# From tile 12 on, k joins r on the block-turned path, and two GpSimd products move to ScalarE

## The chip, the cores and the metric

One Trainium2 chip, one NeuronCore of it. The metric is the device time of one execution in microseconds (us); lower is better. Engines are named as in the profile: PE (TensorE matmuls; PEld its weight loads), DVE (VectorE), ACT (ScalarE), POOL (GpSimd), SP (SyncE, which here only issues DMAs).

## The reference

An RWKV-like attention (batch 4, 8 heads, 768 steps, head size 48) feeds a mixture of 8 experts whose gate is balanced by eight Sinkhorn rounds.

```python
state = 0                                   # per batch and head, 48 x 48
for t in range(768):
    y[t] = r[t] @ (state + (u * k[t]) outer v[t])
    state = w[:, None] * state + k[t] outer v[t]
x = y as (3072, 384)
P = sinkhorn(exp(x @ w_gate - max))         # 3072 x 8
out = sum over e of P[:, e] * (relu(x @ w1[e]) @ w2[e])   # 384 -> 1024 -> 384
```

## The kernel before, in words

The 3072 tokens are 24 tiles of 128; six tiles make one batch entry. The decays are handled in chunks of one tile: r and k are multiplied by tables of powers of w, so that inside a tile attention is a masked product, and between tiles only a state (`sd`, copied into `S`) is handed on.

The main loop runs `for i in range(NTT + 3)`; a pass of it is called iteration i below. In iteration i every engine gets its instructions in program order (each call goes through a wrapper that forbids reordering), and the engines meet only at semaphores. What iteration i issues, in this order:

- loads of k, r, v for tile i+4 on SP (`load_round`); `prep(i+2)`: r and k of tile i+2 times tables, into `rp_` and `kp_`; from tile 12 on (`TX0 = 12`) r takes another way, below;
- `bonus_dot(i+1)`: on POOL, `rk` = r times k, then times u;
- `stage_b(i+1)`: PE turns tile i+1 (four 128x128 transposes each for r and k, tiles `prT`, `pkT`), ACT copies them to `rT`, `kT`;
- `bonus(i)`: DVE sums `rk` by heads into `dg`, POOL forms `av` = v times `dg`;
- `sum_x`, `scale_x(i-2)`: ACT takes the sum of absolute values of the attention output `x`, DVE turns it into a power-of-two scale (`inv_s`, `xs`), ACT writes the high half `xsc`;
- `spread(i-1)`: ACT copies the state `sd` into `S`;
- `work(1)`: one unit of expert 0 on PE, either a `g1` unit (9 matmuls into `ph`; ACT forms the high half of relu, `hb`, and DVE the low half, also `hb`) or a `g2` unit (12 matmuls from `hb` into `po`; ACT copies to `stg`, SP stores it to `e0d`);
- `stage_c(i)`: PE forms scores `pA` from `kT` and `rT`, DVE masks them into `at`; the low half of the unit above comes after that on DVE; PE forms the state's update `pu`, DVE adds it to `sd`, POOL multiplies `sd` by the decay of a tile (`wcb`);
- `low_x(i-2)`: DVE forms the low half of `xsc`, SP transposes it by DMA into `hbx`;
- `work(2)`: two more expert units;
- steps of `combine_tokens` (`prepare`): DVE sums `ws<-hbx`, POOL sums `ws<-ws`, ACT casts and DVE low halves `xv`, four SP copies `xv<-hbx` every six iterations;
- `stage_d(i-1)`: PE forms `py`; `finish(i-1)`: DVE adds `py` and `av` into `x`;
- `load_blocks(i+4)`; `stage_f(i-4)`: PE forms gate logits `px`, ACT copies them to `lparts`.

So the PE order of an iteration is: transposes, unit, `pA`, `pu`, two units, `py`, `px`. PSUM buffers that matter: `ph` has two, `po` and `px` share two (`tag="po"`), and `pA`, `pu`, `py`, `prT`, `pkT` share four.

The other way of r, from tile 12 on: `load_blocks` reads r again by four DMAs (each block of 32 steps twice, shifted) into `rx_`; `turn_r` transposes 32x32 blocks on DVE into `rp_`; `scale_r` multiplies by `tab` on POOL and writes `rT`. There are two `rx_` buffers, and `turn_r` of tile i+2 stands in `prep(i+2)`, early in iteration i.

After the loop come the other seven experts, with fewer matmuls by a 3x3 bilinear scheme (`bA`, `bB`, `bC`, `bY`, `bZ`), and a general path that these inputs do not take.

Of the kernel before, what the change touches and what calls it, by code (L numbers as in the profile page):

```python
# [8 lines left out]
F32 = mybir.dt.float32  # L9
# [3 lines left out]
AF = mybir.ActivationFunctionType  # L13
ALU = mybir.AluOpType
# [19 lines left out]
def rwkv_sinkhorn_moe(  # L34
# [47 lines left out]


    HB = FHC * TH * TB // 2
    hbx = const.tile([P, 3 * HB], F32, name="hbx")
# [238 lines left out]
    RX = GX * D + 32  # L324
    rx_ = [part(hbx, F32, 3 * HB - (2 - i) * NPAIR * RX, (NPAIR, RX)) for i in range(2)]

    def load_blocks(tt):
        b, c = divmod(tt, NCHB)
        src = r[b].rearrange("(p j) (n q g) d -> j n q p (g d)", j=2, g=GX, q=32)
        for j in range(2):  # L330
            for lo in (0, 32):
                rows = slice(HP * j + lo, HP * j + lo + 32)
                Q.dma_start(rx_[tt % 2][rows, :, 32 - lo : 32 - lo + GX * D], src[j, c])
# [84 lines left out]
    tabr, tab = (part(hb3, F32, at_, (NPAIR, C)) for at_ in (1040, HB))  # L418
# [52 lines left out]
    def turn_r(tt):  # L471
        x_ = rx_[tt % 2][:, :, 32:].rearrange("p a (g d) -> p a g d", d=D)[:, :, :, :32]
        V.transpose(rp_[tt % 2].rearrange("p (a j) (g q) -> p a (j g) q", j=2, q=32), x_)

    def scale_r(tt):
        rT = at2.tile([P, NPAIR, P], F32, tag="rT", name=f"rT_{tt}", bufs=3)
        x_ = rp_[tt % 2].rearrange("p (a j) (g q) -> p a q (j g)", j=2, q=32)
        G.tensor_tensor(
            rT.rearrange("p a (q g) -> p a q g", g=GX), x_,
            tab.rearrange("p a (q g) -> p a q g", g=GX), op=ALU.mult,  # L480
        )
        st.setdefault(tt, {})["rT"] = rT

    def prep_r(tt):
        if tt >= TX0:
            turn_r(tt)
            return
        G.tensor_tensor(rp_[tt % 2][:, :, :D], loads[tt]["r"], rt4, op=ALU.mult)

# [30 lines left out]
    def bonus(tt):  # L520
        vn = loads[tt]["v"]
        dg = at2.tile([P, H], F32, tag="dg", name=f"dg_{tt}")
        V.tensor_reduce(dg, st[tt]["rk"], axis=AX.X, op=ALU.add)
        av = st[tt].pop("rk")
        G.tensor_tensor(av, vn, dg.unsqueeze(2).broadcast_to([P, H, D]), op=ALU.mult)
        st[tt]["av"] = av

    def stage_b(tt):
        d = st.setdefault(tt, {})
        for nm, src in (("rT", rp_[tt % 2]), ("kT", kp_[tt % 3]))[tt >= TX0 :]:  # L530
            pt = ps3.tile([P, NPAIR, P], F32, tag="pa", name=f"p{nm}_{tt}")
# [277 lines left out]
    for i in range(NTT + 3):  # L809
        if i == 1:  # L810
            gate_max()
        if i + 2 < NTT:
            if i != 4:
                load_round(i)
            if i:
                if i + 1 >= TX0:
                    scale_r(i + 1)
                prep(i + 2)
        elif i + 1 < NTT:
            scale_r(i + 1)  # L820
# [33 lines left out]
        held[0] = False  # L854
        form_lows()
        if i == 4:
            for x_ in rx_:
                G.memset(x_[:, :, GX * D :], 0.0)
# [20 lines left out]
        planned(i, "c")  # L879
        for _ in range(n_steps(i, 1)):  # L880
            prepare()
        if 1 <= i <= NTT:
            stage_d(i - 1)
            if i > NSUM:
                finish(i - 1)
        if i > NSUM:
            planned(i, "d")
            for _ in range(n_steps(i, 2)):
                prepare()
        if TX0 <= i + 4 < NTT:  # L890
# [586 lines left out]
```

## Time and profile before

| | |
|---|---|
| runs | 1513.76, 1515.78, 1516.59 us; median 1515.78 |
| profiled execution | 1516.68 us, its span 1514.7 us; granted clock 0.999 |
| busy over the span | PE 99%, PEld 56%, DVE 66%, ACT 46%, POOL 37% |
| chain that ended last | PE 95%, DVE 2%, SP's queue 1%, DMA 1% |
| tiles 12 to 23 | iterations 12 to 23: first `pA` at 98.8 us, last `py` ends near 211 us |

All instructions carry one line number (a helper records them), so rows are told apart by engine, tile names and shapes. A row of the timeline reads: start in us, length in us, engine, operation, out<-in, shape, and in brackets how long the engine had been idle and what ended that. A row of groups ends in: busy us, mean ns | idle us before. Spacing between starts is used where instructions of an engine overlap.

### The profile page before, as it was taken

To read this page: it belongs to the slowest core of one execution; us is meant where nothing else is said; L and a number is where in the kernel's file an instruction comes from. 1 tells how busy PE (TensorE), PEld (TensorE's weight loads), DVE (VectorE), ACT (ScalarE), POOL (GpSimd) and SP (SyncE) were. 2 spreads that over 40 slices of the span, in tenths; PEclk is the share of its full clock that TensorE was granted. 3 is DMA by queue.
4 is the path that set the end of the run, shared out by engine and by line. 5 is a ranking of instruction groups with operands and counts; after the bars stand their busy time and mean duration, and the time that the engine had idled before them with its cause. 6 is when DMAs were issued, how large, how long until landed. Compare 5 with 4: busy or idle time off the path is not lost.

```text
span 1514.7 us, 26043 instructions
## 1 busy us (share of the span) xinstructions
PE 1502.9 (99%) x10228; PEld 847.8 (56%) x10228; DVE 995.2 (66%) x1647; ACT 696.9 (46%) x1289; POOL 565.9 (37%) x667
## 2 busy tenths in 40 slices
PE   8999999999999999999999999999999999999998
PEld 6777666555555555555555555555555555555555
DVE  6878759576666666666676666666565666566563
ACT  7645545345354544445454544545353544444320
POOL 8577946200224243342525243242424233242200
PEclk9999999999999999999999999999999999999999
DMA  9776732212255566756666676655554454545434
GB/s 185 163 168 147 142 82 81 83 47 73 82 108 63 83 128 92 126 81 123 91 93 110 89 128 92 118 59 98 61 96 57 60 97 61 95 62 96 57 96 131
DMA packets 193638, 147.69 MB, mean 98 GB/s; under 512 B 110306, under 2 KB 187748, under 8 KB 193508
## 3 DMA queue, kind: packets, MB, share of 16 engines
q0 software_dynamic: 44928, 61.36, 32.7%
q1 hardware_dynamic: 148370, 84.60, 21.1%
q8 instruction: 81, 1.33, 0.4%
q14 instruction: 49, 0.40, 0.1%
q10 hardware_dynamic: 210, 0.00, 0.0%
HBM read 59.92 MB, written 80.23 MB: 93 GB/s over the span
## 4 chain that ended last, share of the span: by engine, by line
PE 95%; DVE 2%; SPq 1%; DMA 1%; ACT 0%; issue 0%; ACTq 0%; DVEq 0%
PE po L30 49%; PE bZ L30 12%; PE bY L30 12%; PE ph L30 6%; PE bA L30 5%; PE bB L30 5%; PE bC L30 2%; PE py L30 2%; PE pA L30 1%; SPq L30 1%; PE pu L30 1%; PE pkT L30 1%; PE px L30 0%; DMA ws<-in_moe_w_dram 0%; DMA hbx<-xsc 0%; DVE wms L30 0%
## 5 line engine op out<-in xcount | busy, mean ns | idle before, releaser
L30 PE MATMUL po<-ws,hbx 128*128 128x384 f16 x3360 | 737.0, 326 | 0.0
L30 POOL DMA_DIRECT2D accd<-stg x288 | 249.7, 867 | 694.9 <-ACT stg L30 670.9
L30 PEld LDWEIGHTS <-hbx 128*128 128x128 f16 x3504 | 333.9, 98 | 295.8 <-DMA hbx<-xsc 2.5
L30 PEld LDWEIGHTS <-ws 128*128 128x128 f16 x3096 | 301.4, 98 | 245.0 <-issue 2.0
L30 ACT ACTIVATE hbx<-tb 128x512 f16<-128x512 f32 x224 | 141.1, 630 | 448.6 <-DVE tb L30 448.6
L30 PE MATMUL po<-ws,hb 128*128 128x384 f16 x1248 | 323.3, 326 | 0.0
L30 DVE TENSOR_TENSOR tb<-bY,tb 128x512 f32<-128x512 f32 x168 | 116.2, 691 | 195.8 <-PE bY L30 195.4
L30 ACT ACTIVATE stg<-po,pe 128x384 f32<-128x384 f32 x312 | 179.2, 574 | 122.4 <-PE po L30 98.0
L30 PE MATMUL bZ<-xv,ws 128*128 128x512 f16 x840 | 227.1, 379 | 0.5 <-DVE tb L30 0.5
L30 PE MATMUL bY<-xv,ws 128*128 128x512 f16 x840 | 227.1, 379 | 0.0
L30 DVE TENSOR_TENSOR tb<-bZ,tb 128x512 f32<-128x512 f32 x168 | 115.6, 688 | 134.7 <-PE bZ L30 134.7
L30 PEld LDWEIGHTS <-hb 128*128 128x128 f16 x1248 | 121.3, 98 | 93.4 <-issue 0.6
L30 POOL TENSOR_TENSOR ucb<-rawb 128x256 f32<-128x256 f32 x84 | 76.9, 966 | 116.5 <-DVE tb L30 78.3
L30 DVE TENSOR_TENSOR tb<-bB,tb 128x512 f32<-128x512 f32 x112 | 77.5, 692 | 49.2 <-PE bB L30 47.3
L30 PE MATMUL ph<-hbx,ws 128*128 128x384 f16 x576 | 104.2, 326 | 0.8 <-DVE hb L30 0.8
L30 DVE SCALAR_TENSOR_TENSOR hb<-tb,hbx 128x512 f16<-128x512 f32 x112 | 77.2, 689 | 24.6 <-ACT hbx L30 19.5
L30 PE MATMUL bA<-xv,ws 128*128 128x512 f16 x336 | 90.8, 379 | 0.0
L30 PE MATMUL bB<-xv,ws 128*128 128x512 f16 x336 | 90.8, 379 | 0.0
L30 DVE SCALAR_TENSOR_TENSOR hbx<-tb,hbx 128x512 f16<-128x512 f32 x112 | 77.3, 691 | 14.6 <-ACT hbx L30 10.4
L30 ACT COPY tb<-bZ 128x512 f32<-128x512 f32 x56 | 32.7, 585 | 65.6 <-PE bZ L30 65.5
L30 DVE SCALAR_TENSOR_TENSOR hb<-ph,hb 128x384 f16<-128x384 f32 x64 | 35.3, 552 | 29.3 <-ACT hb L30 28.8
L30 DVE TENSOR_REDUCE wms<-rawb 128x1 f32<-128x768 f32 x56 | 51.7, 944 | 0.0
(177 smaller groups left out, 1460.9 us busy)
## 6 DMA issues: line engine op xcount, KB each, us to landing
accd<-stg POOLq DMA_DIRECT2D x288, 192.0 KB, 3.6
rawb<-in_moe_w_dram SPq DMA_DIRECT2D x28, 768.0 KB, 7.6
e0d<-stg SPq DMA_DIRECT2D x48, 192.0 KB, 2.1
hb<-e0d SPq DMA_DIRECT2D x48, 192.0 KB, 3.7
vn<-in_v_dram SPq DMA_DIRECT2D x24, 192.0 KB, 3.4
hbx<-in_r_dram SPq DMA_DIRECT2D x48, 96.0 KB, 2.8
accd<-stg SPq DMA_DIRECT2D x24, 192.0 KB, 1.8
accd<-hb POOLq DMA_DIRECT2D x24, 192.0 KB, 4.7
```

The lines of the kernel that those rows point to most:

```text
L30: return lambda *a, **k: self.tc.keep_in_program_order(f(*a, **k))
```

## The change

From tile 12 on:

- k too is loaded by blocks (twice, four DMAs), turned on DVE, and given its decays by a POOL product that writes `kT`; PE's transposes `pkT` and ACT's copy of them are gone. `rtab`, no longer needed as such by then, takes the table for k (one ACT multiplication in iteration 10).
- `rx_` holds k and r of one tile instead of r of two tiles; `load_blocks` is called for tile i+3 instead of i+4, at the same place of iteration i; both turns of tile i+2 stand in front of `stage_d(i-1)` instead of early in iteration i.
- `av`, v times the bonus sums, is formed by eight ACT instructions (one a head) ahead of `stage_f`, instead of one POOL product.
- the state's decay is applied by four ACT instructions in `spread`, in front of the copies into `S`, instead of one POOL product behind DVE's sum. This concerns `sd` of tiles 13 to 16 and 19 to 22.

```diff
-    def turn_r(tt): ...
-    def scale_r(tt): ...
+    def turn():
+        for dst, x_ in zip(rp_, rx_):
+            V.transpose(dst..., x_[:, 32:]...[:, :, :, :32])
+
+    def scale_turned(tt):
+        for nm, src, t_, n in zip(("kT", "rT"), rp_, (rtab..., tab), (2, 3)):
+            dst = at2.tile([P, NPAIR, P], F32, tag=nm, name=f"{nm}_{tt}", bufs=n)
+            G.tensor_tensor(dst..., src..., t_..., op=ALU.mult)
...
+    def bonus_heads(tt):
+        d = st[tt]
+        d["av"] = av = d.pop("rk")
+        for h in range(H):
+            S_.activation(av[:, h], loads[tt]["v"][:, h], AF.Copy, scale=d["dg"][:, h : h + 1])
...
     def stage_b(tt):
+        if tt >= TX0:
+            return
...
-                G.tensor_tensor(sd, sd, wcb, op=ALU.mult)
+                if tt < TX0:
+                    G.tensor_tensor(sd, sd, wcb, op=ALU.mult)
...
+            if tt >= TX0 and tt % NCHB:
+                for p_ in range(NPAIR):
+                    s_ = sd_[tt % 2][:, p_]
+                    S_.activation(s_, s_, AF.Copy, scale=wc[:, p_ : p_ + 1])
...
+        if TX0 <= i + 2 < NTT:
+            turn()
         if 1 <= i <= NTT:
             stage_d(i - 1)
...
-        if TX0 <= i + 4 < NTT:
-            load_blocks(i + 4)
+        if TX0 <= i + 3 < NTT:
+            load_blocks(i + 3)
+        if TX0 <= i < NTT:
+            bonus_heads(i)
         if 4 <= i:
             stage_f(i - 4, bank_)
```

DVE from the low half `xv` at the end of iteration 15 to the head sums `dg` of iteration 16 (`ws<-hbx` are the sums of `combine_tokens`, `STREAM_TRANSPOSE` is a turn); before:

```order
L30 TENSOR_TENSOR xv_76<-ws_74,xv_76 128x4x256
L30 TENSOR_TENSOR x_2282<-py_2257,rk_1862 128x384
L30 TENSOR_TENSOR ws_74<-hbx 128x2x3x128 x2
L30 STREAM_TRANSPOSE rp_157<-hbx 128x512
L30 TENSOR_TENSOR kp_159<-kn_1995,ktab 128x8x48
L30 TENSOR_REDUCE dg_2317<-rk_2154 128x8
```

The same stretch of DVE, changed:

```order
L30 TENSOR_TENSOR xv_76<-ws_74,xv_76 128x4x256
L30 STREAM_TRANSPOSE rp_157<-hbx 128x512
L30 STREAM_TRANSPOSE rp_158<-hbx 128x512
L30 TENSOR_TENSOR x_2312<-py_2287,rk_1879 128x384
L30 TENSOR_TENSOR ws_74<-hbx 128x2x3x128 x2
L30 TENSOR_TENSOR kp_159<-kn_2017,ktab 128x8x48
L30 TENSOR_REDUCE dg_2353<-rk_2187 128x8
```

There are two turns instead of one, and both stand ahead of `x` and of everything of the next iteration.

ACT from the cast at the end of iteration 15 to the first relu `hb` of iteration 16; before:

```order
L30 CAST xv_76<-ws_74 128x4x256
L30 ACTIVATE lparts<-px_2254,inv_s 128x16
L30 COPY kT_2315<-pkT_2310 128x512
L30 ACTIVATE xsc_2321,xm_2320<-x_2282 128x384
L30 ACTIVATE xsc_2321<-x_2282,xs_2323 128x384
L30 COPY S_165<-sd_167 64x4x48 x2
L30 ACTIVATE hb_73<-ph_2_2330 128x384
```

The same stretch of ACT, changed:

```order
L30 CAST xv_76<-ws_74 128x4x256
L30 ACTIVATE rk_2028<-vn_1575,dg_2190 128x48 x8
L30 ACTIVATE lparts<-px_2282,inv_s 128x16
L30 ACTIVATE xsc_2356,xm_2355<-x_2312 128x384
L30 ACTIVATE xsc_2356<-x_2312,xs_2358 128x384
L30 ACTIVATE sd_167<-sd_167,wc 128x48 x4
L30 COPY S_165<-sd_167 64x4x48 x2
L30 ACTIVATE hb_73<-ph_2_2369 128x384
```

Eight small instructions stand ahead of `lparts`, four ahead of the copies into `S` and so ahead of the relu; the copy into `kT` is gone.

SP's queue at the end of iteration 10, where the four copies `xv<-hbx` stand; before:

```order
L30 DMA e0d_80<-stg_0_1_1500 128x384
L30 DMA xv_76<-hbx 128x2x128 x4
L30 DMA hbx<-in_r_dram 32x4x192 x4
L30 DMA kn_1562<-in_k_dram 128x8x48
L30 DMA rn_1564<-in_r_dram 128x8x48
```

The same stretch of SP's queue, changed:

```order
L30 DMA e0d_80<-stg_0_1_1503 128x384
L30 DMA xv_76<-hbx 128x2x128 x4
L30 DMA hbx<-in_k_dram 32x4x192 x4
L30 DMA hbx<-in_r_dram 32x4x192 x4
L30 DMA kn_1571<-in_k_dram 128x8x48
L30 DMA rn_1573<-in_r_dram 128x8x48
```

Eight block loads stand there instead of four, and they are for tile 13 instead of tile 14.

More of the change, by code (lines that the diff above doesn't have):

```diff
@@ L84, in rwkv_sinkhorn_moe @@
     HB = FHC * TH * TB // 2
-    hbx = const.tile([P, 3 * HB], F32, name="hbx")
+    hbx = const.tile([P, 3 * HB + 32], F32, name="hbx")
     hb3 = const.tile([P, HB + 2 * DM], F32, name="hb3")
@@ L322, in load_part @@
         loads.setdefault(tt, {})[nm] = t_
-    RX = GX * D + 32
-    rx_ = [part(hbx, F32, 3 * HB - (2 - i) * NPAIR * RX, (NPAIR, RX)) for i in range(2)]
+    RX = NPAIR * GX * D
+    rx_ = [part(hbx, F32, 3 * HB - (2 - i) * RX, (RX + 32,)) for i in range(2)]
     def load_blocks(tt):
         b, c = divmod(tt, NCHB)
[L329 to L333, printed above, removed]
+        for x_, all_ in zip(rx_, (k, r)):
+            src = all_[b].rearrange("(p j) (n q g) d -> j n q p (g d)", j=2, g=GX, q=32)
+            for j in range(2):
+                for lo in (0, 32):
+                    rows = slice(HP * j + lo, HP * j + lo + 32)
+                    Q.dma_start(
+                        x_[rows, 32 - lo : 32 - lo + RX].rearrange("p (a d) -> p a d", d=GX * D), src[j, c]
+                    )
     raws = (part(ws0, F32, 0, (KC, F)), part(ws0, F32, KC * F, (FC, DM)))
@@ L417, in rwkv_sinkhorn_moe @@
     )
-    tabr, tab = (part(hb3, F32, at_, (NPAIR, C)) for at_ in (1040, HB))
+    tab = part(hb3, F32, HB, (NPAIR, C))
+    tabr = part(hbx, F32, 3 * HB - 2 * RX - NPAIR * C, (NPAIR, C))
     S_.copy(tab[:, :, HP:], pw[:, :, :HP])
@@ L469, in rwkv_sinkhorn_moe @@
     kt4 = ktab.rearrange("p a j d -> p (a j) d")[:, :, :D]
[L471 to L482, printed above, removed]
+    def turn():
+        for dst, x_ in zip(rp_, rx_):
+            V.transpose(
+                dst.rearrange("p (a j) (g q) -> p a (j g) q", j=2, q=32),
+                x_[:, 32:].rearrange("p (a g d) -> p a g d", g=GX, d=D)[:, :, :, :32],
+            )
+    def scale_turned(tt):
+        for nm, src, t_, n in zip(("kT", "rT"), rp_, (rtab.rearrange("p a j d -> p a (j d)"), tab), (2, 3)):
+            dst = at2.tile([P, NPAIR, P], F32, tag=nm, name=f"{nm}_{tt}", bufs=n)
+            G.tensor_tensor(
+                dst.rearrange("p a (q g) -> p a q g", g=GX),
+                src.rearrange("p (a j) (g q) -> p a q (j g)", j=2, q=32),
+                t_.rearrange("p a (q g) -> p a q g", g=GX), op=ALU.mult,
+            )
+            st.setdefault(tt, {})[nm] = dst
     def prep_r(tt):
         if tt >= TX0:
-            turn_r(tt)
             return
@@ L523, in bonus @@
         V.tensor_reduce(dg, st[tt]["rk"], axis=AX.X, op=ALU.add)
-        av = st[tt].pop("rk")
-        G.tensor_tensor(av, vn, dg.unsqueeze(2).broadcast_to([P, H, D]), op=ALU.mult)
-        st[tt]["av"] = av
+        st[tt]["dg"] = dg
+        if tt < TX0:
+            av = st[tt].pop("rk")
+            G.tensor_tensor(av, vn, dg.unsqueeze(2).broadcast_to([P, H, D]), op=ALU.mult)
+            st[tt]["av"] = av
+    def bonus_heads(tt):
[3 more added lines that the diff above has]
+            S_.activation(av[:, h], loads[tt]["v"][:, h], AF.Copy, scale=d["dg"][:, h : h + 1])
     def stage_b(tt):
+        if tt >= TX0:
+            return
         d = st.setdefault(tt, {})
-        for nm, src in (("rT", rp_[tt % 2]), ("kT", kp_[tt % 3]))[tt >= TX0 :]:
+        for nm, src in (("rT", rp_[tt % 2]), ("kT", kp_[tt % 3])):
             pt = ps3.tile([P, NPAIR, P], F32, tag="pa", name=f"p{nm}_{tt}")
@@ L575, in stage_c @@
                 V.tensor_tensor(sd, pu, sd_[(tt - 1) % 2], op=ALU.add)
-                G.tensor_tensor(sd, sd, wcb, op=ALU.mult)
+                if tt < TX0:
+                    G.tensor_tensor(sd, sd, wcb, op=ALU.mult)
     def spread(tt):
@@ L816, in rwkv_sinkhorn_moe @@
                 if i + 1 >= TX0:
-                    scale_r(i + 1)
+                    scale_turned(i + 1)
                 prep(i + 2)
         elif i + 1 < NTT:
-            scale_r(i + 1)
+            scale_turned(i + 1)
         if i + 1 < NTT and i:
@@ L824, in rwkv_sinkhorn_moe @@
             stage_b(i + 1)
+        if i == TX0 - 2:
+            S_.mul(rtab.rearrange("p a j d -> p a (j d)"), tabr, rows_used)
         planned(i, "s")
@@ L856, in rwkv_sinkhorn_moe @@
         if i == 4:
-            for x_ in rx_:
-                G.memset(x_[:, :, GX * D :], 0.0)
+            G.memset(rx_[1][:, RX:], 0.0)
+            rows_used = ac.tile([P, 1], F32, name="rows_used")
+            G.memset(rows_used, 0.0)
+            for j in range(2):
+                G.memset(rows_used[j * HP : j * HP + D], 1.0)
             load_round(i, "rk")
```

## The prediction

> **What bounds the kernel now.** I read the page first, then PE's waits in the stage that the change touches, then the timelines of DVE and ACT there.
>
> ```profile
> PE 1502.9 (99%) x10228; PEld 847.8 (56%) x10228; DVE 995.2 (66%) x1647; ACT 696.9 (46%) x1289; POOL 565.9 (37%) x667
> ...
> PE ph L30 <- DVE hb L30: 0.8, 1, 0.8
> ...
> 150.00:180.00 30.00, 30.00 (x431) 21.00 (x427) 24.32 (x47) 15.00 (x35) 29.29 (x31) 1.00 0.87 174
> ```
>
> The first row says that PE is busy for 99% of the span. The next heads the list of PE's waits between 60 and 330 us: 0.8 us, once. The last is a stretch of the stage (PE, PEld, DVE, ACT, POOL, clock, DMA share, GB/s): PE never stops, but POOL is busy for 29.3 of 30 us, DVE for 24.3, and the DMA engines for 0.87 of the time. So PE sets the pace, and the others have little to spare. Work taken off PE pays only as far as they follow.
>
> **What PE gives up.** The transposes of k, four a tile, for tiles 12 to 23:
>
> ```profile
> 186.45 0.31 PE L30 MATMUL px<-wgp,hbx 128*128 128x16 f16 x6
> 186.61 0.64 PE L30 MATMUL pkT<-ident,kp 128*128 128x128 f32 x4
> 187.08 2.11 PE L30 MATMUL po<-ws,hb 128*128 128x384 f16 x12
> ...
> 196.01 0.31 PE L30 MATMUL px<-wgp,hbx 128*128 128x16 f16 x6
> 196.18 1.62 PE L30 MATMUL ph<-hbx,ws 128*128 128x384 f16 x9
> ```
>
> With `pkT`, the next unit starts 0.63 us after `px`; without it (tile 24 doesn't exist) 0.17 us after. The lengths overlap; the place itself is 187.08 - 186.61 = 0.47 us. Twelve of them are 5.6 us, and that is all PE can gain. The profiled execution took 1516.68 us (its span and 2.0 us around it), 0.9 us over the median of 1515.78, to which I apply the sum.
>
> **What the others get.** Durations from groups over 100 to 210 us (the last two numbers before the bar's end are busy us, mean ns):
>
> ```profile
> L30 DVE STREAM_TRANSPOSE rp<-hbx 128x512 f32<-128x512 f32 x9 | 6.3, 702 | 1.2 <-POOL ws L30 0.6 <-DMA hbx<-in_r_dram 0.6
> L30 DVE TENSOR_TENSOR kp<-kn,ktab 128x384 f32<-128x384 f32 x9 | 8.1, 896 | 0.0
> L30 POOL TENSOR_TENSOR rT<-rp,hb 128x512 f32<-128x512 f32 x11 | 18.0, 1632 | 2.8 <-PE py L30 2.8
> L30 POOL TENSOR_TENSOR rk<-vn,dg 128x384 f32<-128x384 f32 x12 | 11.5, 957 | 1.0 <-DVE inv_s L30 1.0
> L30 POOL TENSOR_TENSOR sd<-sd,wcb 128x192 f32<-128x192 f32 x8 | 5.8, 720 | 4.2 <-DVE sd L30 3.2 <-ACT stg L30 1.0
> L30 ACT ACTIVATE xsc<-x,xs 128x384 f16<-128x384 f32 x13 | 8.0, 616 | 24.7 <-DVE xs L30 24.7
> L30 ACT CAST xv<-ws 128x768 f16<-128x768 f32 x5 | 4.2, 832 | 0.1
> L30 ACT CAST xv<-ws 128x1024 f16<-128x1024 f32 x2 | 2.1, 1046 | 0.1
> ```
>
> - POOL: 12 products `kT` at 1.63 (as `rT`) are +19.6; 12 `av` at 0.96 and 8 `sd` at 0.72 go, -17.2. Net +2.4 us over twelve iterations. `kT` and `rT` of tile i+1 are formed in iteration i and read by `pA` an iteration later, so I cost POOL at nothing; without that cover `kT`'s 1.6 us would stand in front of `pA`.
> - DVE: one turn more a tile. Starts below are 0.63 apart, so +0.63 an iteration.
> - ACT: the two casts give 214 ns for 256 elements, 0.84 ns each; `xsc`, which also scales by a column, comes down from 616 ns at 384 elements to 335 at 48, and its successor starts 0.09 before its end (139.86 + 0.61 against 140.38 below). So 0.245 each: 1.96 for the heads, 0.98 for four pairs of the state. The smallest bound is half of that, the largest 335 ns unoverlapped, 1.3 for four. The heads stand in front of `lparts`, behind which ACT waits for DVE's `x` anyway, beside `xv` and the two turns (1.88 and 1.26 in iteration 15, below); hidden. The copy into `kT` that goes stood in the same cover and saves nothing. The state's four are not, as follows.
>
> **Where it lands on PE.** Iteration 15 into 17, one chain over ACT and DVE beside PE:
>
> ```profile
> 131.17 0.48 ACT L30 COPY stg<-po 128x384 f32<-128x384 f32 x1 [1.50 <-PE po L30]
> ...
> 132.75 0.31 PE L30 MATMUL px<-wgp,hbx 128*128 128x16 f16 x6
> 132.75 1.88 DVE L30 TENSOR_TENSOR xv<-ws,xv 128x1024 f16<-128x1024 f32 x1 [2.49 <-ACT xv L30]
> ...
> 137.56 0.70 DVE L30 STREAM_TRANSPOSE rp<-hbx 128x512 f32<-128x512 f32 x1
> 138.19 0.72 DVE L30 TENSOR_TENSOR kp<-kn,ktab 128x384 f32<-128x384 f32 x1
> ...
> 139.86 0.61 ACT L30 ACTIVATE xsc<-x,xs 128x384 f16<-128x384 f32 x1 [4.06 <-DVE xs L30]
> 140.38 0.71 ACT L30 COPY S<-sd 64x192 f32<-64x192 f32 x2
> ...
> 141.63 0.56 DVE L30 SCALAR_TENSOR_TENSOR hb<-ph,hb 128x384 f16<-128x384 f32 x1 [0.54 <-ACT hb L30]
> ...
> 142.47 1.62 PE L30 MATMUL ph<-hbx,ws 128*128 128x384 f16 x9
> ```
>
> DVE's `xv` is followed by `x`, the sums, a turn, `kp`, the scale; then ACT does `xsc`, `S` and the relu, and only after the relu DVE forms the low half `hb`, done at 142.19. That frees a `ph` buffer (there are two, and three `ph` units follow each other here), and PE's next `ph` starts at 142.47: 0.28 us to spare, which no list of waits shows. From `xv` to 142.19 it is 9.44 us, from `px` to `ph` 9.72. After the change the chain has a second turn (+0.63) and the four state instructions (+0.98), 11.05 us; PE has two `pkT` less, 8.78. PE waits 2.3 us.
>
> And the chain comes in late. Each iteration adds 0.63 + 0.98 on DVE and ACT and takes 0.47 from PE, 2.08 together (1.10 into iteration 13, which has no state to scale). ACT's spare time is its waits for PE:
>
> ```profile
> 113.14 0.49 ACT L30 ACTIVATE hb<-ph 128x384 f16<-128x384 f32 x1 [0.94 <-PE ph L30]
> ...
> 121.56 0.49 ACT L30 ACTIVATE hb<-ph 128x384 f16<-128x384 f32 x1 [0.97 <-PE ph L30]
> ```
>
> These are iterations 13 and 14; iteration 15 has 1.50 (`stg` at 131.17). The lateness is 1.10 - 0.94 = 0.16, then 0.16 + 2.08 - 0.97 = 1.27, then 1.27 + 2.08 - 1.50 = 1.85. With it PE waits 4.1 us at the start of iteration 17. Bounds 2.3 and 4.1; I take 4.1, since each addend is a row.
>
> In iteration 22 `px` needs the buffer that this copy empties:
>
> ```profile
> 193.52 0.48 ACT L30 COPY stg<-po 128x384 f32<-128x384 f32 x1
> ```
>
> It ends at 194.00, `px` starts at 196.01: 2.0 us to spare. Two turns (that iteration had none) and four state instructions cost 1.26 + 0.98, PE is 0.47 earlier: a wait of 0.7. Lateness by the same count for iterations 19 to 21 adds up to 1.3. Bounds 0.7 and 2.0, taken 2.0.
>
> **DMA.** The block loads double, and they come an iteration later:
>
> ```profile
> 90.13 2.71 SPq L30 DMA_DIRECT2D xv<-hbx  x4
> 92.89 2.03 SPq L30 DMA_DIRECT2D hbx<-in_r_dram  x4
> ...
> hbx<-in_r_dram SPq DMA_DIRECT2D x36, 96.0 KB, 2.9
> ...
> 96.80 0.56 DVE L30 TENSOR_TENSOR x<-py,rk 128x384 f32<-128x384 f32 x1 [2.68 <-PE py L30]
> ...
> 100.74 0.47 ACT L30 ACTIVATE hb<-ph 128x384 f16<-128x384 f32 x1
> ...
> 101.92 2.11 PE L30 MATMUL po<-ws,hb 128*128 128x384 f16 x12
> ```
>
> Four issues hold SP for 2.0 us, so tile 13's eight run from 92.9 to 96.9; the last is issued at 96.4 and lands 2.9 later, at 99.3. Its turn sits in front of `x` on DVE, which ran at 96.8, when `py` came. Behind the waiting turn queue `x`, `kp`, the scale and ACT's relu: from `x` to the relu's end it was 4.4 us, a turn of 0.63 in it, so 99.3 + 0.6 + 3.8 = 103.7 instead of 101.2. The `po` at 101.92 (0.94 earlier by then) needs that relu at its tenth matmul of twelve, 1.5 us in, at 102.5: PE waits 1.2 us, or nothing if the loads land a little sooner than the median. Iteration 19 has the same form two iterations behind the second group of `xv` copies, and in iteration 18 the first `po` waits for a buffer that ACT empties late. Bounds for each of the three 0 and 1.6 (a lateness as before iteration 16); I take 0.9 each, 2.7, nearer to the 1.2 than to nothing. SP also runs past these issues with `kn`, `rn`, `vn` and the transposes of `xsc`; those are read two iterations later and cost nothing unless SP falls a whole iteration behind (a rival).
>
> **The sum.** -5.6 + 4.1 + 2.0 + 2.7 = +3.2 us: 1515.8 + 3.2 = 1519.0. The stage after the loop starts from PE's last unit and moves along whole.
>
> **The rivals.** A difference under 0.2% (3.0 us) can't be told from no change here.
>
> - *All is absorbed.* The additions to DVE and ACT lie beside the chain, not on it. Even then PE, earlier by 0.94 with 0.28 to spare, waits 0.7: -5.6 + 0.7 = -4.9, 1510.9. For it: PE waits for almost nothing now. Against it: both the turn and the state's scaling stand on the queue between two rows of the chain. 0.12.
> - *Only the bare chains.* No lateness is carried and the loads land in time: -5.6 + 2.3 + 0.7 = -2.6, 1513.2. It decides for "not slower" as soon as the carried lateness and the loads together stay below 2.6 us. DVE ends several of these iterations behind PE already, and may catch up where a step has no `xv`. 0.27.
> - *SP and the DMA engines become the bound.* After the second group, SP ran without a pause:
>
> ```profile
> 156.09 2.46 SPq L30 DMA_DIRECT2D hbx<-in_r_dram  x4
> ...
> 163.80 3.46 SPq L30 DMA_DIRECT2D hbx<-in_r_dram  x4
> ```
>
>   A period of 7.7 us, with four issues stretched to 2.5 to 3.5. Four more make 10.2 to 11.2, against 9.1 on PE (186.45 to 196.01, less 0.47). Over iterations 17 to 20 that is 4.4 to 8.4, say 6.4, in place of the 2.7: -5.6 + 4.1 + 2.0 + 6.4 = +6.9, and some more if the first group does the same: 1523. 0.15.
> - *POOL's longer presence slows DVE.* The product `kp` took 1.47 us, ending 0.41 after POOL's `rT`, which had started before it:
>
> ```profile
> 124.49 1.53 POOL L30 TENSOR_TENSOR rT<-rp,hb 128x512 f32<-128x512 f32 x1
> 124.96 1.47 DVE L30 TENSOR_TENSOR kp<-kn,ktab 128x384 f32<-128x384 f32 x1
> ```
>
>   After the change `kp` follows the turns by one instruction, just when POOL starts `kT`. At 1.47 instead of the mean of 0.90 in eleven tiles, DVE's round grows by 6.3 us on the same chain: 1525. Against it: POOL is nearly always busy now, so the mean already holds such waits. 0.10. The Trainium skill (SBUF — State Buffer, "SBUF: two separate sides") says that a GpSimd instruction and a VectorE one with two SBUF inputs lock the same read port for a whole instruction, and the later one is blocked. These two rows agree with it; by that rule alone, with every `kp` caught, this rival would be the forecast.
>
> That the change doesn't do what it says has no chance worth a number: without `pkT` nothing but `kT` from POOL can feed `pA`.
>
> **How the numbers follow.** The forecast has 0.36, its own range 1516.5 to 1521.5 (with 0 or 1.6 at the three places). Faster by over 0.2% (below 1512.8): all of the first rival and 0.12 of the second, 0.24. Within 0.2%: 0.15 of the second and 0.14 of the forecast, 0.29. Slower: 0.22 of the forecast and the last two rivals, 0.47. The range goes from 1511.0, which leaves out half of the first rival, to 1524.0, which leaves out half of the last two.
>
> **What would show it.** PE's busy time in `pkT` halves, and its waits grow from nothing to some 9 us, the longest at a `ph` on DVE's `hb` near 140 us, one at a `px` or `po` on ACT's `stg` near 196. DVE should show idle time on ACT in front of `hb` of 1.5 instead of 0.54, and on DMA in front of a turn in iterations 11, 12 and 17 to 19. ACT's small instructions should be spaced by 0.245. I am wrong if PE still waits nowhere, or if the waits are DVE's turns on DMA in every iteration.

## The result, and the profile after

The changed kernel took 1534.19 us (median; 1532.56 to 1535.73) beside 1515.59 for the kernel before on the same chip: a ratio of 1.0129, 95% interval 1.0117 to 1.0141, so 17.7 to 21.4 us slower. The forecast was 1519.0, with a range of 1511.0 to 1524.0. The profiled execution took 1534.96 us. From `px` of iteration 10 to `px` of iteration 24 TensorE needed 123.23 us before (87.65 to 210.88) and 140.97 after (87.69 to 228.66). I call this the stage; all but 1 us of the loss lies in it. A kernel further down with the same work in the same order had 141.90, so stages compare to about 1 us.

The page's first row (busy us, share, instructions of each engine), then the list of what PE waited for between 60 and 330 us (total, times, longest):

```profile
PE 1503.6 (98%) x10180; PEld 845.4 (55%) x10180; DVE 1010.7 (66%) x1659; ACT 718.4 (47%) x1406; POOL 566.2 (37%) x661
```

```profile
PE po L30 <- ACT hb L30: 6.5, 2, 5.2
PE ph L30 <- DVE hb L30: 5.2, 2, 4.4
PE px L30 <- ACT stg L30: 4.8, 3, 3.1
PE po L30 <- ACT stg L30: 1.1, 1, 1.1
```

These rows sum to 17.6 us (1.3 of it also stood in the list before); before, a wait of 0.8 us headed the list. PE's busy time did not fall by the 5.6 us of `pkT`; it rose by 0.7, though 48 matmuls fewer ran. PE's timeline shows why (the bracket is the wait ahead of a row):

```profile
107.84 1.15 PE L30 MATMUL po<-ws,hb 128*128 128x384 f16 x3 [5.20 <-ACT hb L30]
108.92 1.55 PE L30 MATMUL py<-S,rT 128*64 128x96 f32 x16
...
145.43 0.88 PE L30 MATMUL py<-S,rT 128*64 128x96 f32 x16
...
151.89 3.06 PE L30 MATMUL ph<-hbx,ws 128*128 128x384 f16 x9 [4.43 <-DVE hb L30]
...
157.88 1.63 PE L30 MATMUL ph<-hbx,ws 128*128 128x384 f16 x9
...
171.48 0.29 PE L30 MATMUL px<-wgp,hbx 128*128 128x16 f16 x6 [1.16 <-ACT stg L30]
...
179.26 0.93 PE L30 MATMUL po<-ws,hb 128*128 128x384 f16 x3 [1.34 <-ACT hb L30]
...
212.19 0.29 PE L30 MATMUL px<-wgp,hbx 128*128 128x16 f16 x6 [3.12 <-ACT stg L30]
212.34 2.48 PE L30 MATMUL ph<-hbx,ws 128*128 128x384 f16 x9
```

These are the places of the forecast: iteration 12, 17, 18 (there at `px`, not at the first `po`), 19 and 22; one it did not name is a wait of 1.09 us in iteration 21 (the fourth row of the list). But behind the three long waits the same matmuls take nearly twice as long: `py` 1.55 us at 108.92 and 0.88 at 145.43, `ph` 3.06 at 151.89 and 1.63 at 157.88. Short stretches (length, then PE, PEld, DVE, ACT, POOL busy, clock, DMA share, GB/s) name the cause in the clock column:

```profile
109.00:110.00 1.00, 1.00 (x14) 1.00 (x16) 1.00 (x2) 0.93 (x4) 1.00 (x2) 0.50 1.00 206
...
113.00:114.00 1.00, 1.00 (x5) 0.46 (x4) 1.00 (x3) 0.45 (x2) 1.00 (x2) 0.52 0.71 139
114.00:115.00 1.00, 1.00 (x17) 0.56 (x18) 0.37 (x3) 0.53 (x2) 1.00 (x2) 1.00 1.21 237
...
152.00:153.00 1.00, 1.00 (x4) 0.47 (x4) 1.00 (x3) 0.97 (x6) 0.00 (x0) 0.50 0.05 8
...
213.00:214.00 1.00, 1.00 (x5) 0.48 (x4) 1.00 (x3) 1.00 (x5) 0.00 (x0) 0.50 0.72 230
...
216.00:217.00 1.00, 1.00 (x19) 0.64 (x12) 0.42 (x2) 0.88 (x3) 0.92 (x3) 0.82 0.00 0
```

By stretches of one us, the granted clock is 0.50 behind the three waits until 114.0, 154.9 and 216.4 (there from 213.0 on): 6.1, 3.0 and 3.4 us of work at half speed, so 3.1, 1.5 and 1.7 us longer. The waits of 1.1 to 1.3 us have no such tail. In the trace itself the clock is 0.50 for 6.83, 3.42 and 3.41 us (107.14 to 113.97, 151.51 to 154.93, 212.95 to 216.36): once or twice 3.41 us, and the starts too lie whole multiples of 3.41 us apart.

Where the wait of iteration 12 comes from, on the timelines of SP, DVE and ACT:

```profile
91.06 2.70 SPq L30 DMA_DIRECT2D xv<-hbx  x4
93.87 3.01 SPq L30 DMA_DIRECT2D hbx<-in_k_dram  x4
96.97 1.80 SPq L30 DMA_DIRECT2D hbx<-in_r_dram  x4
...
100.87 1.30 DVE L30 STREAM_TRANSPOSE rp<-hbx 128x512 f32<-128x512 f32 x2 [5.00 <-DMA hbx<-in_r_dram]
...
102.54 1.52 DVE L30 TENSOR_TENSOR xv<-ws,xv 128x768 f16<-128x768 f32 x1
103.98 1.87 DVE L30 TENSOR_TENSOR kp<-kn,ktab 128x384 f32<-128x384 f32 x1
...
107.31 0.85 ACT L30 ACTIVATE hb<-ph 128x384 f16<-128x384 f32 x2
```

DVE stands 5.00 us in front of the turns for tile 13's blocks. `x` and everything behind it waits with them, and ACT's relu, which PE needs, starts at 107.31. And into iteration 17:

```profile
139.72 1.23 DVE L30 TENSOR_TENSOR xv<-ws,xv 128x1024 f16<-128x1024 f32 x1 [0.88 <-ACT xv L30]
140.86 1.30 DVE L30 STREAM_TRANSPOSE rp<-hbx 128x512 f32<-128x512 f32 x2
...
142.52 3.73 DVE L30 TENSOR_TENSOR ws<-hbx 128x768 f32<-128x768 f16 x2
146.17 1.35 DVE L30 TENSOR_TENSOR kp<-kn,ktab 128x384 f32<-128x384 f32 x1
...
148.99 0.99 ACT L30 ACTIVATE sd<-sd,wc 128x48 f32<-128x48 f32 x4
...
151.28 0.56 DVE L30 SCALAR_TENSOR_TENSOR hb<-ph,hb 128x384 f16<-128x384 f32 x1 [1.61 <-ACT hb L30]
```

This is the chain that was forecast, with its second turn, the four scalings (0.99 us) and DVE's idle time ahead of `hb` (1.61, forecast 1.5). One row in it was not forecast to change, the two sums `ws`, 3.73 us here. Before, they took

```profile
135.02 2.62 DVE L30 TENSOR_TENSOR ws<-hbx 128x768 f32<-128x768 f16 x2
```

### The profile page after: what moved, and what is told of

It reads as the page before. It is cut to its first block, busy times and chain, and to the rows that moved or that the text cites. A ratio compares the mean times of both kernels' runs of the same rounds, so it can differ in the third digit from the quotient of the medians.

```text
span 1533.4 us, 26153 instructions
## 1 busy us (share of the span) xinstructions
PE 1503.6 (98%) x10180; PEld 845.4 (55%) x10180; DVE 1010.7 (66%) x1659; ACT 718.4 (47%) x1406; POOL 566.2 (37%) x661
## 4 chain that ended last, share of the span: by engine, by line
PE 87%; DVE 5%; DMA 3%; SPq 2%; ACT 1%; issue 1%; POOL 0%; DVEq 0%; POOLq 0%; ACTq 0%
PE po L30 46%; PE bZ L30 12%; PE bY L30 12%; PE bA L30 5%; PE bB L30 5%; PE ph L30 4%; PE bC L30 2%; SPq L30 2%; DMA hbx<-in_r_dram 1%; PE py L30 1%; DVE kp L30 1%; DVE rp L30 1%; DVE ws L30 1%; PE pA L30 1%; DVE xv L30 0%
## 5 line engine op out<-in xcount | busy, mean ns | idle before, releaser
L30 PE MATMUL ph<-hbx,ws 128*128 128x384 f16 x576 | 107.3, 333 | 5.2 <-DVE hb L30 5.2
```

The lines of the kernel that those rows point to most:

```text
L30: return lambda *a, **k: self.tc.keep_in_program_order(f(*a, **k))
```

## The experiments

My theory was that blocks which land late and a longer DVE-ACT chain make the waits, and that the half clock comes on top. Rivals: GpSimd slowing DVE, the prediction's fourth rival (`kp` at 1.47 us beside `rT`); ACT's twelve small instructions by themselves; late engines alone, with the half clock costing nothing of its own. Ratios are to the kernel before, run on the same chip; the stage is that of the one profiled execution. What lies ahead of the stage varies on its own (it starts between 83.5 and 87.7 us, whatever the edit), so ratio and stage need not move by the same amount.

| edit of the changed kernel | ratio (95%) | stage, us |
|---|---|---|
| none | 1.0129 (1.0117 to 1.0141) | 140.97 |
| `load_blocks` written earlier (same order on SP) | 1.0115 (1.0098 to 1.0132) | 141.90 |
| idle work at three places | 1.0164 (1.0147 to 1.0181) | 150.88 |
| the same, placed anew | 1.0114 (1.0097 to 1.0131) | 138.61 |
| idle work at two places | 1.0099 (1.0085 to 1.0114) | 140.12 |
| no product `kT` | 1.0118 (1.0101 to 1.0135) | 142.34 |
| separate buffers of k and r | 1.0108 (1.0093 to 1.0124) | 141.30 |
| copies behind the blocks | 1.0109 (1.0092 to 1.0126) | 137.55 |
| k alone | 1.0091 (1.0074 to 1.0108) | 133.06 |
| two sets of blocks | 1.0067 (1.0051 to 1.0084) | 134.54 |
| state first | 1.0051 (1.0035 to 1.0068) | 132.92 |
| state first, copies behind the blocks | 1.0058 (1.0041 to 1.0075) | 131.38 |
| state first, two sets (A) | 1.0036 (1.0024 to 1.0047) | 127.65 |
| A, copies at the end | 1.0006 (0.9997 to 1.0015) | 122.99 |
| A, k by blocks to tile 20 only | 1.0032 (1.0021 to 1.0044) | 122.11 |
| A, both of these | 0.9987 (0.9978 to 0.9996) | 120.62 |
| the last, sums later | 0.9986 (0.9977 to 0.9995) | 118.95 |
| *before*, only `av` on ACT | 0.9996 (0.9986 to 1.0006) | 123.22 |
| *before*, only the state's decay on ACT | 1.0003 (0.9993 to 1.0013) | 124.04 |

### Parts alone, on the kernel before and without the others

```diff
 # before
+        for h in range(H):
+            S_.activation(av[:, h], loads[tt]["v"][:, h], AF.Copy, scale=d["dg"][:, h : h + 1])
```

> The kernel before with only av moved to ScalarE (eight instructions, 1.9 us an iteration). If they hide in front of lparts, as I had it: within 1 us of the kernel before. If they too stand on the chain (lparts, xsc and relu come behind them): 2 to 6 us slower.

```diff
 # before, in spread
+            if tt >= TX0 and tt % NCHB:
+                for p_ in range(NPAIR):
+                    S_.activation(s_, s_, AF.Copy, scale=wc[:, p_ : p_ + 1])
```

> The kernel before with only the state's decay moved to ScalarE, behind xsc (four instructions, 0.99 us, eight iterations). By my chain (0.28 us to spare at iteration 17): a wait of 0.7 there and little elsewhere, 0.5 to 2 us slower. If it is hidden: no change. If each such iteration pays it: 8 x 0.99 = 7.9 us slower.

Neither costs any time that can be measured. With the state's decay alone, PE's timeline at iteration 17 has the one wait that the chain gives, 0.99 less 0.28 to spare (forecast 0.7):

```profile
139.18 1.62 PE L30 MATMUL ph<-hbx,ws 128*128 128x384 f16 x9 [0.65 <-DVE hb L30]
```

```diff
 # after
-                if tt < TX0:
-                    G.tensor_tensor(sd, sd, wcb, op=ALU.mult)
+                G.tensor_tensor(sd, sd, wcb, op=ALU.mult)
 # and av back on G
```

> The changed kernel with both products back on GpSimd: av from dg, and the state's decay behind VectorE's sum; only k's loads, turn and product remain of the change. If the four scalings on ScalarE's chain are what the waits at 17 and 22 come from: as with the state first, 1524 to 1526. If it is the loads and the added turn: 1532 to 1534. If GpSimd (29.3 of 30 us busy before, now 0.8 more an iteration net of nothing given up) becomes the bound: 12 products of 1.5 us, 18 us more than before, 1534 or later, with waits for kT or av on POOL.

k by itself makes it slower by 0.74 to 1.08%. The waits at 17 and 22 fall to 2.69 and 0.33 us and the time to 1526.8, near the first of the three cases, so the scalings made part of them; GpSimd, with more to do than in the changed kernel, is not the bound. What stays is 9.8 of the stage's 17.7 us: k's new path is the larger part. ACT's part, which costs nothing on the kernel before, costs here where DVE and ACT are late already.

### Where the state's scaling stands

```diff
+        if TX0 < i < NTT:
+            spread(i - 1)
         if 2 <= i <= NTT + 1:
             if i - 2 >= NSUM:
                 sum_x(i - 2)
...
-        if 1 <= i < NTT:
+        if 1 <= i < NTT and i <= TX0:
             spread(i - 1)
```

> The changed kernel with spread(i-1), ScalarE's four scalings of the state and two copies into S, in front of sum_x (where ScalarE idles for VectorE's x) from iteration 13 on, instead of behind xsc and ahead of relu. If the lengthened ScalarE-VectorE chain makes the waits at iterations 17 and 22: 0.99 + 0.72 = 1.7 us off both, the waits become 2.7 and 1.4, too short for the half clock behind them (1.5 and 1.6): -6.5 us, 1528, while the wait of 5.2 in iteration 12 stays. If late blocks (DMA) or GpSimd's port make them: within 2 us of 1534.

More came back than either theory said: 0.8% of the ratio, 8 us of the stage. In front of `sum_x` ACT idles for DVE's `x`, so 1.7 us (scaling and the copies, which stood in the chain before too) are free there. The wait at 22 goes from 3.12 to 0.34, with its half clock; the one in iteration 12 stays at 5.68, and at 17 it is

```profile
147.77 3.06 PE L30 MATMUL ph<-hbx,ws 128*128 128x384 f16 x9 [2.68 <-DVE hb L30]
```

2.68 us, still followed by `ph` at half speed (3.06): I had taken a wait of 2.7 us to be too short for the half clock, and it is not. The stage and the waits at 12, 17 and 22 are those of k alone, which has neither part of the change on ACT (132.92 and 133.06 us; 5.68, 2.68 and 0.34 beside 5.69, 2.69 and 0.33): with the state first, ACT's instructions cost nothing in the stage. Why the ratio of k alone is still 0.4% higher was not traced; in the profiled executions 1.8 us lie ahead of the stage.

### The blocks' time

```diff
         if TX0 <= i + 2 < NTT:
             turn()
+        if TX0 <= i + 3 < NTT:
+            load_blocks(i + 3)
```

> The changed kernel with load_blocks right behind the turns, so ahead of the four copies xv<-hbx (2.7 us) in SP's queue. If late blocks make the wait in iteration 12: the turn's wait for DMA goes from 5.0 to about 2.1 us, TensorE's 5.2 to about 2.3, without half clock behind it (3.1): -6.0 us, 1528; if VectorE and ScalarE are the bound over the whole stage, TensorE only arrives earlier at iteration 17 and its 4.4 there grows by up to that, 1533 to 1534.

A miss: the copies `xv<-hbx` are issued ahead of the turns, so SP's order stayed, and the run is a repeat of the changed kernel (5.89 us at iteration 12). The next one moves the copies themselves:

```diff
+        while copies:          # behind load_blocks; the four DMAs xv<-hbx
+            copies.pop()()
```

> The changed kernel with the four copies xv<-hbx behind the block loads in SP's queue instead of ahead of them (iterations 10 and 16), which the edit of load_blocks' place did not do: it left SP's order as it was. If late blocks make the wait in iteration 12: the turn waits 5.0 - 2.7 = 2.3 us for its blocks, TensorE 5.2 - 2.7 = 2.5, and 0 to 3.1 us of half clock go too: 1528.5 to 1531.5. If VectorE and ScalarE are the bound over the stage, TensorE waits the longer at iteration 17: 1533 to 1534.

```profile
102.74 0.50 PE L30 MATMUL po<-ws,hb 128*128 128x384 f16 x2 [3.12 <-ACT hb L30]
...
146.70 3.06 PE L30 MATMUL ph<-hbx,ws 128*128 128x384 f16 x9 [5.09 <-DVE hb L30]
```

PE's wait of iteration 12 falls to 3.12, this time with the full clock behind it (two matmuls in 0.50), but the one at 17 grows to 5.09. 3.4 us of the stage come back; the ratio's interval overlaps that of the changed kernel, so in time no gain is shown.

```diff
-    hbx = const.tile([P, 3 * HB + 32], F32, name="hbx")
+    hbx = const.tile([P, 3 * HB + 64], F32, name="hbx")   # rx_[0], rx_[1] apart
```

> The changed kernel with 32 columns more, so that the block buffers of k and r don't overlap and k's turn needn't wait for r's blocks, nor r's loads for k's turn. If the shared columns tie them: one turn (0.65 us) goes ahead of the wait in each late iteration, 0.5 to 3 us less, 1531 to 1533.5. If not: as the changed kernel, 1533 to 1535.

k's turn now goes 2.2 us ahead of r's, but waits 4.91 itself, for k's own blocks. The interval overlaps that of the changed kernel, and the stage is the same: no part that can be shown.

```diff
+    rxs_ = [[...], [...]]               # two sets of k and r in hbx
-        if TX0 <= i + 3 < NTT:
-            load_blocks(i + 3)
+        if TX0 <= i + 4 <= 20:
+            load_blocks(i + 4)          # tiles 12 to 20: a set each, by turns
+        if 21 <= i + 3 < NTT:
+            load_blocks(i + 3)          # the other set's place is taken by x from tile 16 on
```

> The changed kernel with two sets of blocks for tiles 12 to 20, loaded one iteration earlier (load_blocks(i+4), as for r before); tiles 21 to 23 keep one set. If one set is too tight (issue of eight loads 3.7 us, 2.6 to 3.2 to the landing, turns 1.3: 7.6 to 8.2 of TensorE's 8.6 an iteration, before any copy or store stands in SP's queue): VectorE's turns wait for no DMA up to tile 20, the 5.2 us in iteration 12 and the half clock behind it go (8 us), and 2 to 5 of that come back at iteration 17: 1526 to 1531. If the DMA engines themselves are too slow for twice the blocks: the waits stay, 1533 to 1535.

PE's waits in that kernel:

```profile
141.25 3.06 PE L30 MATMUL ph<-hbx,ws 128*128 128x384 f16 x9 [3.69 <-DVE hb L30]
...
177.83 0.88 PE L30 MATMUL py<-S,rT 128*64 128x96 f32 x16 [2.38 <-DVE x L30]
182.96 3.13 PE L30 MATMUL po<-ws,hb 128*128 128x384 f16 x12 [3.10 <-ACT stg L30]
...
203.99 0.29 PE L30 MATMUL px<-wgp,hbx 128*128 128x16 f16 x6 [1.81 <-ACT stg L30]
204.14 2.85 PE L30 MATMUL ph<-hbx,ws 128*128 128x384 f16 x9
```

The wait of iteration 12 is gone, and iterations 12 to 16 are 0.46 to 0.48 us shorter than before each; at 1524.6 us the kernel is a little faster than the first theory's range. The first wait is now the forecast one: 3.69 at iteration 17, where I had 4.1. The others stand in iterations 20 to 22; tiles 21 to 23 have one set.

### Both, and what was left

> The changed kernel with both repairs: the state's scaling and its copies ahead of sum_x, and the copies xv<-hbx behind the block loads. If the two causes are separate: 1524.1 (state first alone) less 2.7 of wait and 0 to 3.1 of half clock in iteration 12, 1518.3 to 1521.4. If the first wait only gives TensorE's time to a later one: 1523 to 1524.

In time this gives nothing over the state first alone (1.0058 beside 1.0051), as the second theory has it, and 1.5 us in the stage. Iteration 12 waits 3.37 instead of 5.68 and iteration 17 still 2.40, but the copies of the second group now stand ahead of tile 20's loads in SP's queue, which runs without a pause there, and iteration 19 waits 2.38 instead of 0.86.

> Two sets of blocks and the state's scaling ahead of sum_x together. If late blocks and the lengthened ScalarE chain are all that is wrong: the waits of 5.7 (iteration 12) and 2.7 (iteration 17) shrink to 0 and 1 to 3, and the kernel reaches 1512 to 1517, about the kernel before. If VectorE's added turn and GpSimd's longer hold of the shared port are the bound: VectorE is late at iteration 17 whatever comes earlier, 1519 to 1523.

At 1518.6 us this lies between the two theories. To iteration 18 only one wait is left (1.55 us at 17). Then SP and DVE show what remains:

```profile
145.08 3.60 SPq L30 DMA_TRANSPOSE hbx<-xsc  x1
148.77 0.54 SPq L30 DMA_DIRECT2D e0d<-stg  x1
149.35 2.63 SPq L30 DMA_DIRECT2D xv<-hbx  x4
152.08 2.97 SPq L30 DMA_DIRECT2D hbx<-in_k_dram  x4
155.15 1.80 SPq L30 DMA_DIRECT2D hbx<-in_r_dram  x4
...
159.25 1.30 DVE L30 STREAM_TRANSPOSE rp<-hbx 128x512 f32<-128x512 f32 x2 [5.50 <-DMA hbx<-in_r_dram]
```

SP issues in order: blocks stand behind a transpose that takes DVE's `xsc` (3.60 us here, 1.2 to 1.8 mostly), a store that takes ACT's `stg`, and the copies. So late engines can make late blocks, and late blocks make late engines.

```diff
+        if i >= 21 and copies:
+            copies.pop(0)()             # instead of iterations 10 and 16
```

> State first, two sets of blocks, and the copies xv<-hbx (2.7 us of SP each time) moved from iterations 10 and 16 to iterations 21 and 22, where no blocks are loaded any more. If the copies are what makes the blocks late from iteration 18 on: the turns' waits of 5.5 and 6.2 us fall by 2.7 or more each, TensorE's 3.0 in iteration 19 goes with its half clock, 1513.5 to 1516. If the single set for tiles 21 to 23 does it: no change, 1517 to 1519.

```diff
+    TX1 = 21                            # k of tiles 21 to 23: pkT on PE; r alone by blocks
-        if TX0 <= i + 4 <= 20:
+        if TX0 <= i + 4 < NTT:
             load_blocks(i + 4)
```

> State first, two sets of blocks up to tile 20, and tiles 21 to 23 as in the kernel before (k turned by TensorE, r alone by blocks, loaded two iterations ahead); 9 places of 0.47 us are saved instead of 12 (4.2). If the single set does it: the waits from iteration 19 on go, what is left is about 1.5 at iteration 17 and 3 at 18 to 20: 1514 to 1516. If the copies do it: iteration 19 still waits 3 us with its half clock, 1517 to 1519.

> Both of the last two: two sets for tiles 12 to 20, tiles 21 to 23 as before, the copies at the end, the state first. If lateness of blocks is all that is left: 4.2 us gained, 1.5 lost at iteration 17, 1512 to 1514 beside a kernel before of 1515.5. If VectorE's added turn and GpSimd's product hold it: 1515 to 1518.

Each alone leaves waits besides the 1.5 us at iteration 17: with the copies at the end 1.75 and 1.31 in iterations 20 and 21; with k to tile 20 0.95 in iteration 19, where the profiled execution (1512.49) was the fastest of its seven runs, the others up to 1523. Together they make a kernel that is faster than before, by 0.04 to 0.22%, just clear of the noise. Its one new wait is 1.51 at iteration 17, and the last run removes that:

```diff
+        if j == 2 and i in (15, 18, 19):
+            return 0 if i == 15 else 3   # steps of combine_tokens: none in 15 (2 before), 3 in 18 and 19
```

> As the last (state first, two sets up to tile 20, k of tiles 21 to 23 on TensorE, copies at the end), with the two sums ws of iteration 15's second half taken an iteration later (3.8 us of VectorE between two low halves hb). If VectorE's load makes the wait at iteration 17: it goes, 1.5 us, 1511 to 1512 beside 1515.2 of before. If the sums only move it: 1512.5 to 1514.

The list of PE's waits of that kernel has again, as before the change, one row in front of the two that were always there:

```profile
PE ph L30 <- DVE hb L30: 0.8, 1, 0.8
```

The stage is 118.95, 4.28 less than before: nine places of 0.476. Of that the timed runs show only 0.05 to 0.23%, no more than with the wait: the wait is gone, as the first theory has it, but the time (1512.7 beside 1514.1) is that of the second. The profiled execution (1511.11) was the third fastest of eleven, up to 1514.40, so the others may have waits that it has not; why they give less than its stage stays open.

### GpSimd and the port

```diff
-        for nm, src, t_, n in zip(("kT", "rT"), rp_, (rtab..., tab), (2, 3)):
+        for nm, src, t_, n in (("rT", rp_[1], tab, 3),):
 # and turn() writes k's blocks into kT
```

> The changed kernel without GpSimd's product kT: VectorE's turn of k writes kT itself, so k goes without its decays into the scores (that part of the computation is left out) and GpSimd has 12 products of 1.5 us less. If GpSimd's hold on the port that VectorE shares is the main cause: kp falls from 1.35-1.87 to 0.6-0.9, xv and ws too, about 1 us of VectorE an iteration, and 9 us or more come back: 1525 or below. If it is late blocks, the added turn and the four scalings: the waits of 5.2, 4.4 and 3.1 shrink by 0.5 to 1 each, 1531 to 1533, unless one falls under some 3 us and loses its half clock too (1.5 more).

No change. The group rows of `kp` (count, then busy us and mean ns) over 100 to 210 us, in the changed kernel, in this one, and in the kernel with two sets of blocks:

```profile
L30 DVE TENSOR_TENSOR kp<-kn,ktab 128x384 f32<-128x384 f32 x10 | 12.7, 1267 | 0.0
```

```profile
L30 DVE TENSOR_TENSOR kp<-kn,ktab 128x384 f32<-128x384 f32 x10 | 14.7, 1466 | 0.0
```

```profile
L30 DVE TENSOR_TENSOR kp<-kn,ktab 128x384 f32<-128x384 f32 x9 | 9.1, 1009 | 0.0
```

`kp` was 896 ns before. The turns now stand just ahead of it and release GpSimd's product at that moment (into iteration 17 the turns start at 140.86 and `kT`, which had waited for them, at 141.71); without `kT`, `kp` meets `rT` instead (ahead of iteration 17 the sums `ws` still take 3.80 us and `kp` 1.35). So the stretch is real, and it does not come from the added product. That it comes from the turns' place is not shown either: with two sets of blocks the turns stand at the same place and GpSimd has all twelve products, and `kp` is at 1009. No run took the overlap with GpSimd itself away, so its share of the waits stays open.

### The half clock

```diff
+            if now[0] == 12 and fl == FHC - 1:
+                idle_work(pw_[:, DM:], 72)     # matmuls of 128 columns, unread
...                                             # the other places likewise, 64 and 44
```

> The changed kernel with idle work for TensorE: 72, 64 and 44 matmuls of 128 columns (0.056 us each: 4.0, 3.6 and 2.5 us), whose results nobody reads, at the three places where it waited 5.20, 4.43 and 3.12 us. They are shorter than the waits, so nothing is put later. Theory A (each of these waits costs twice: its length, and the half clock behind it): the clock stays at 1.00 at 108-114, 152-155 and 213-216 us, and 3.1 + 1.5 + 1.6 = 6.2 us go: 1528. Theory B (the half clock costs nothing by itself, since ScalarE and VectorE are late anyway and TensorE would only wait for them later): the clock stays up, the waits at the other places grow by as much, 1534.

> Again idle work for TensorE at the three long waits of the changed kernel (72, 64, 44 matmuls of 128 columns, 0.056 us each, results unread), now put so that only the first waits for nothing but TensorE itself: in iteration 12 inside the unit that waited 5.20; behind px of iteration 16 in a buffer of its own; in iteration 22 behind the last matmul of the unit ahead of py. In the first attempt the clock stayed at 1.00 in iteration 12 and TensorE was 1.9 us earlier by px of iteration 16; the other two places were spoilt by new waits of 9.2 and 5.5 us. Theory A (the half clock behind a long wait is paid on top of the wait): 1.9 + 1.5 + 1.6 = 5.0 us go, 1529. Theory B (it is not, ScalarE and VectorE are behind anyway): 1534.

> The changed kernel with idle work for TensorE only at the two places where it did not make a wait of its own: 72 matmuls of 128 columns inside the unit of iteration 12, 44 behind the last unit of iteration 22 (results unread). Theory A (the half clock behind a wait is paid on top of the wait): 2.9 + 1.6 = 4.5 us go, 1529 to 1530 at the times of before of 1515. Theory B (TensorE waits as much longer elsewhere): within 1.5 us of the changed kernel, 1532.5 to 1534.

The idle work changes the values of the units whose bank it shares; no instruction of theirs is left out. At iteration 17 both attempts waited for a reader of their own bank (9.22 and 5.85 us), so that place was not tried cleanly. In iteration 12 the clock stayed up in all three kernels, and behind iteration 22 in the second and third; in the first the idle work at 22 itself waited 5.45 us. PE and the clock in the last of the three:

```profile
105.85 0.98 PE L30 MATMUL po<-ws,hb 128*128 128x384 f16 x3 [1.70 <-ACT hb L30]
...
150.29 3.04 PE L30 MATMUL ph<-hbx,ws 128*128 128x384 f16 x9 [6.57 <-DVE hb L30]
...
210.47 0.29 PE L30 MATMUL px<-wgp,hbx 128*128 128x16 f16 x6 [0.67 <-ACT stg L30]
210.62 1.62 PE L30 MATMUL ph<-hbx,ws 128*128 128x384 f16 x9
```

```profile
102.00:106.00 4.00, 2.30 (x40) 2.09 (x38) 3.93 (x9) 1.20 (x3) 3.92 (x4) 1.00 0.86 186
...
211.00:214.00 3.00, 3.00 (x45) 1.90 (x44) 2.34 (x5) 2.76 (x12) 1.66 (x3) 1.00 0.71 197
```

What PE won in iterations 12 and 13 (1.9 us) it waited at 17, 6.57 instead of 4.43, and at 18, 2.18 instead of 1.16. Behind iteration 22 nothing is late any more, and the win stays: iteration 23 takes 7.98 us instead of 9.61. The timed difference, 0.3% to the changed kernel and 0.16% to its repeat, is unclear between the theories; this trace says that the half clock costs its full price only where no late engine is met afterwards: 1.6 us behind iteration 22, next to nothing behind iteration 12.

## Why the prediction was wrong

Right: the direction, though the +3.2 us of the forecast were hardly more than the 3.0 I called too small to tell; the gain (0.47 a place; iterations without waits are 0.47 to 0.48 shorter); the prices of ACT's instructions (0.99 and 1.91 us, forecast 0.98 and 1.96); the place at 22; that the eight heads are hidden (shown on the kernel before).

In the stage, 14.5 us were missed: 17.7 lost, 3.2 forecast. By the rows of the profile that is 5.0 in the three places of the DMA part, 0.3 at iteration 17, 1.1 at 22, 1.1 in iteration 21, where no wait was forecast, and 6.3 of half clock; 0.7 are left over. As a wait that goes can come back further on, this says where the time lies, not what each part alone is worth.

The step that failed is the DMA part, "I take 0.9 each, 2.7": the three places measured 5.20, 1.16 and 1.34, together 7.7. In iteration 12, to my 1.2 us come 1.5 because the blocks landed at 100.87 instead of 99.3, 0.6 because both turns waited, not one, and 1.9 because `xv` and `kp` behind them were stretched beside GpSimd's products (starts 1.44 and 1.79 apart, before 0.87 and 0.44): 5.2. The blocks landed later because SP came to them at 93.87, not at 92.89 (up to tile 12's blocks, at 81.8, it ran as before; they are eight loads instead of four), and k's four issues took 3.01 behind the copies, not 2.03. I had bounded each place by 1.6, the lateness before iteration 16; a wait for data has no such bound. Under it lies what I did not count: the loop through one set of blocks. Issue 3.7, landing 1.7 to 3.9 after the last issue and turns 1.3 are 6.7 to 8.9 us of an iteration of 7.9 to 9.1, before SP has waited for anything.

The second is `px` of iteration 22: 3.12, my upper bound was 2.0. The lateness there came from the blocks and from the state's place on ACT; with the state first it was 0.34.

The third is a term that was missing, the half clock. The Trainium skill (TensorE: Matmul & The Clock Gate, "HAM oscillation — how this bites in real kernels") warns of idle gaps of TensorE over about 3.4 us, after which its clock is halved; my own 4.1 us should have called that up. The traces agree in kind, not in the length: 2.68 us and once 1.81 (with two sets, ahead of `px` of iteration 22, `ph` 2.85 behind it) were enough here, and 3.12 once was not.

That the wait at iteration 17 came out at 4.43 where I had 4.1 is in part luck, for two errors cancel. The lateness that I carried into the chain, 1.85, was 1.16 (`xv` starts at 139.72, `px` at 138.56). From `xv` to the end of `hb` I had 11.05 us and it took 12.12, as the sums `ws` were 1.1 longer and `kp` 0.6, and `xv` 0.7 shorter. With two sets the lateness is 0.2, the chain 12.4, and the wait 3.69: the bare chain is worth over a microsecond more than my 2.3.

The rivals: SP and the DMA engines as the bound was the nearest in mechanism, as two sets and relieved copies show, but I gave it 6.4 us and put it mainly behind the second group of copies. GpSimd stretches DVE by 0.37 us a `kp` and 1.1 in the sums ahead of iteration 17 (3.73, before 2.62), yet taking its added product away gave nothing back. That all is absorbed came true for each ACT part alone, but for 0.65 us. A slip: with 0 or 1.6 at the three places my sum gives 1516.3 to 1521.1, not 1516.5 to 1521.5.

## What to carry to other kernels

Work that is moved onto a busy stage costs by its place, not by its length: the same four scalings and two copies cost nothing where ScalarE waits anyway, and 8 us of the stage where a late chain passes through them. For a buffer that is loaded anew each iteration, add up issue, landing and use against the period, with whatever stands ahead in that queue; if little is left, a second set is worth trying early (here it gave back 6.4 us of the stage). And when a forecast says that TensorE will wait for 2 us or more, price the half clock behind it, and ask whether a late engine further on gives it back.

## What the runs showed of the hardware

- TensorE's clock after a wait: 1.00 behind those up to 1.79 us, 0.50 behind one of 1.81 and those from 3.37 up, either between (3.12 us left it at 1.00 once and halved it twice).
- The trace's clock record explains the spread. Within a run every change of the clock in and around the stage lies a whole multiple of 3.41 us from the others, so time falls into fixed stretches of that length. Between 60 and 235 us of all these runs, a full-clock stretch with under 1.3 us of TensorE work was always followed by one at half clock, one with over 2.1 us never; between, both occur. The wait of 3.12 us that left the clock up lay across two stretches, with 1.80 and 1.74 us of work. A halved stretch lasts 3.41 us, or twice that (with idle work once three times), and loses 1.7 us for each 3.41 in which TensorE has work.
- Four block loads took SP 1.8 us in most iterations, and 2.0 to 3.5 right behind the four copies.
- DVE's product `kp` (128x384, two inputs in SBUF) took 0.51 us where it started just ahead of GpSimd's product (98.76 before, GpSimd 98.77), and 1.87 where it started inside one (103.98 in the changed kernel, GpSimd 103.21 to 105.43).
